# Decode attention with a gated MLP: gate moved into the attention output, MLP part summed in PSUM, result gathered on 8 partitions and stored by two transfers, last weight piece halved

## The chip, the cores and the metric

The kernel runs on one core of one Trainium2 chip. The metric is the time of one execution in device microseconds (us), as a median of several. In the trace of one execution the span is about 1.8 us shorter than that time (190.2 for 191.94 us, for example). A ratio is the mean time of one kernel's fast runs over the mean of the fast runs of the kernel before of the same rounds, on the same chip; so it is not quite the ratio of the medians that are quoted beside it. The interval after a ratio is a 95% one. "Same" means within 2%.

## The reference

Eight sequences decode one token each. One input row x gives a gate, an attention result over the last 1024 positions of a key and value cache, and an MLP result; the output mixes the two.

```python
def reference(A_x, A_k_cache, A_v_cache, A_wq, A_wo, B_x, B_w1, B_b1, B_w2, B_b2, gate_w):
    x = A_x                                               # [8, 1, 448], bf16
    g = _sigmoid((x * gate_w).sum(-1, keepdims=True))     # one number per sequence
    a = _A_ref(x, A_k_cache, A_v_cache, A_wq, A_wo)       # attention: 16 heads of 256, 8 kv heads,
                                                          # then o [8, 4096] @ wo [4096, 448]
    b = _B_ref(x, B_w1, B_b1, B_w2, B_b2)                 # layernorm, 448 -> 1792, gelu, -> 448
    return g * a + (1 - g) * b
```

## The kernel before

All large inputs (77.7 MB) stream through a ring of nine landing buffers of 128 partitions x 16,384 bytes. SP issues all these loads. The buffers lie in SBUF behind the pool of constants, so each tile added to that pool moves them.

```python
    WO_PARTS = [[(0, NJ8)]] * (NHQ - 1) + [[(0, 4), (4, 6), (6, 8)]]
    ...
    consts = ctx.enter_context(tc.tile_pool(name="consts", bufs=1))
    ring = ctx.enter_context(tc.tile_pool(name="ring", bufs=RING))      # RING = 9, SLOT = 8192 bf16
    ...
    def pump():
        while len(slots) < min(len(plan), consumed[0] + RING):
            t = ring.tile([P, SLOT], BF16, tag="slot", name="slot")
            plan[len(slots)](t)
            slots.append(t)
```

The last load is the output projection `wo`; its last quarter comes in the pieces that `WO_PARTS` names, so that only a small piece is left when the stream ends. The result has 8 rows and 448 columns. The projection uses four column tiles of the matmul array at once: block i of 112 columns appears on partitions 32i to 32i+7 of one PSUM tile.

```python
    def tiles(ps):
        return [
            (ps[32 * i : 32 * i + NB, :], slice(i * DO, (i + 1) * DO))   # NB = 8, DO = 112
            for i in range(OT)                                           # OT = 4
        ]
    ...
    nc.vector.memset(A_ps[:], 0.0)
    ...
    def project(q):
        w = slot("wo", q - q % 2)
        for j in range(NJ8):
            o = ((q % 2) * NJ8 + j) * D
            for dst, cols in tiles(A_ps):
                nc.tensor.matmul(dst, lhsT=oP[:, j, q, :], rhs=w[:, o + cols.start : o + cols.stop],
                                 start=(q == 0 and j == 0), stop=(q == NHQ - 1 and j == NJ8 - 1))
    ...
    nc.vector.scalar_tensor_tensor(          # res = A_ps * gate + mixb, all 128 partitions at once
        res[:], in0=A_ps[:], scalar=gg_s[:, 0:1], in1=mixb[:], op0=ALU.mult, op1=ALU.add)
    for i, (src, cols) in enumerate(tiles(res)):
        eng = nc.sync if i % 2 == 0 else nc.scalar
        eng.dma_start(out_f[:, cols], src)   # four stores of 8 rows x 224 bytes, two a queue
```

`mixb` holds (1 - g) times the MLP result, ready long before the end.

## Time and profile before

| | before |
|---|---|
| time, median | 192.38 us (first three runs), 192.34 us (six runs) |
| load queue | 77.67 MB, 96.7% of the time of 16 DMA engines |
| last weight piece usable by the matmul engine (PE) | 186.55 us |
| last store landed | 189.13 us |
| end of the span | 190.17 us |

The first fence is from the profile page of the kernel before: the share of time that the DMA engines were busy and their rate, in 40 equal slices of the span; then the queues (packets, MB, share of 16 engines' time); then the shares of the chain of waits that ended last.

```profile
DMA  5999999999999999999999999999999999999990
GB/s 194 413 424 428 426 431 433 427 420 427 427 434 420 431 417 441 424 424 434 424 431 429 424 420 438 424 427 424 427 434 434 420 420 431 431 431 420 409 373 26
...
q1 hardware_dynamic: 6512, 77.67, 96.7%
q8 instruction: 8, 0.13, 0.3%
...
q14 instruction: 4, 0.03, 0.0%
...
DMA 77%; PE 12%; DVE 7%; SPq 1%; ACT 1%; issue 1%
```

The loads run at a constant rate from the second slice to the end, and the chain is mostly DMA. So the time is the load stream, plus what comes after its last byte. The Trainium skill, "DMA: Bandwidth & Descriptors", section "Where 436 GB/s comes from", gives 435.2 GB/s as the ceiling of the path into SBUF; this trace, at some 427 GB/s, agrees.

The second fence is the timeline of the end: start, duration, engine, line, operation, and in brackets the idle time before it and what ended it.

```profile
186.55 0.36 PE L671 MATMUL A_ps<-slot,oP 128*8 128x112 bf16 x8 [0.21 <-DMA slot<-in_A_wo_dram]
186.55 0.10 PEld L671 LDWEIGHTS <-oP 128*8 128x8 bf16 x7 [0.40 <-issue]
186.96 0.33 DVE L689 SCALAR_TENSOR_TENSOR res<-A_ps,gg_s,mixb 128x112 bf16<-128x112 f32 x1 [3.73 <-PE A_ps L671]
187.32 0.71 SPq L699 DMA_DIRECT2D out_dram<-res  x2
187.33 0.65 ACTq L699 DMA_DIRECT2D out_dram<-res  x2
```

After the last weight piece come 8 matmuls, one operation on VectorE (DVE), and two store issues on each of two queues. The third fence is the same kernel's waits of SP's queue at the end (total, times, longest).

```profile
SPq L725 <- DMA out_dram<-res: 1.1, 2, 0.9
```

SP waited 0.9 us for a store's landing at the end.

### The profile page before, as it was taken

To read this page: it belongs to the slowest core of one execution; us is meant where nothing else is said; L and a number is where in the kernel's file an instruction comes from. 1 tells how busy PE (TensorE), PEld (TensorE's weight loads), DVE (VectorE), ACT (ScalarE), POOL (GpSimd) and SP (SyncE) were. 2 spreads that over 40 slices of the span, in tenths; PEclk is the share of its full clock that TensorE was granted. 3 is DMA by queue.
4 is the path that set the end of the run, shared out by engine and by line. 5 is a ranking of instruction groups with operands and counts; after the bars stand their busy time and mean duration, and the time that the engine had idled before them with its cause. 6 is when DMAs were issued, how large, how long until landed. Compare 5 with 4: busy or idle time off the path is not lost.

```text
span 190.2 us, 2502 instructions
## 1 busy us (share of the span) xinstructions
PE 128.5 (68%) x1013; PEld 67.1 (35%) x1022; DVE 128.0 (67%) x186; ACT 43.1 (23%) x91; POOL 5.0 (3%) x7
## 2 busy tenths in 40 slices
PE   0037799896848775796669874848396839687572
PEld 0021783442413342344234433324142414244261
DVE  7866256798949494949494949495868677685300
ACT  2030230034030404040403140404022400335200
POOL 8100000000000000000000000000000000000000
PEclk9999999999996999699975999999799987999555
DMA  5999999999999999999999999999999999999990
GB/s 194 413 424 428 426 431 433 427 420 427 427 434 420 431 417 441 424 424 434 424 431 429 424 420 438 424 427 424 427 434 434 420 420 431 431 431 420 409 373 26
DMA packets 6734, 77.85 MB, mean 409 GB/s; under 512 B 945, under 2 KB 1346, under 8 KB 1986
## 3 DMA queue, kind: packets, MB, share of 16 engines
q1 hardware_dynamic: 6512, 77.67, 96.7%
q8 instruction: 8, 0.13, 0.3%
q10 hardware_dynamic: 210, 0.02, 0.1%
q14 instruction: 4, 0.03, 0.0%
HBM read 77.68 MB, written 0.01 MB: 409 GB/s over the span
## 4 chain that ended last, share of the span: by engine, by line
DMA 77%; PE 12%; DVE 7%; SPq 1%; ACT 1%; issue 1%
DMA slot<-in_A_k_cache_dram 40%; DMA slot<-in_A_v_cache_dram 20%; DMA slot<-in_A_wo_dram 10%; DMA slot<-in_A_wq_dram 7%; PE S L428 6%; DVE kt L356 5%; PE hT L553 2%; PE hT L543 1%; DVE mx L440 1%; SPq L118 1%; SPq L134 1%; PE Sq L370 1%; PE qt L385 1%; ACT qs L380 1%; PE qp L398 1%
## 5 line engine op out<-in xcount | busy, mean ns | idle before, releaser
L356 DVE STREAM_TRANSPOSE kt<-slot 128x2048 int32<-128x2048 int32 x32 | 73.7, 2306 | 34.4 <-DMA slot<-in_A_k_cache_dram 34.4
L428 PE MATMUL S<-kt,qw 128*128 128x512 bf16 x256 | 70.2, 421 | 34.5 <-DVE kt L356 30.1
L428 PEld LDWEIGHTS <-qw 128*128 128x128 bf16 x256 | 26.5, 104 | 71.9 <-issue 51.1
L457 ACT ACTIVATE E<-S,nmx 128x1024 bf16<-128x1024 f32 x16 | 22.2, 1387 | 2.5 <-DVE nmx L454 2.5
L533 ACT CAST oT<-fin 128x16 bf16<-128x16 f32 x16 | 3.6, 226 | 78.7 <-PE fin L530 78.7
L440 DVE TENSOR_REDUCE mx<-S 128x1 f32<-128x1024 f32 x16 | 19.0, 1187 | 1.2 <-PE S L428 1.2
L500 PE MATMUL PO<-slot,ET 128*16 128x512 bf16 x256 | 18.3, 410 | 1.4 <-DMA slot<-in_A_v_cache_dram 1.4
L509 ACT ACTIVATE first<-PO,own 128x256 f32<-128x256 f32 x16 | 7.6, 473 | 28.2 <-PE PO L500 28.2
L470 DVE STREAM_TRANSPOSE ET<-E 128x512 int32<-128x512 int32 x16 | 11.2, 698 | 2.2 <-ACT E L457 2.2
L422 PE MATMUL S<-place,foreign 128*128 128x512 bf16 x23 | 9.2, 400 | 0.1
L448 PE MATMUL mz<-m,same 128*128 128x4 f32 x32 | 6.2, 265 | 4.1 <-ACT oT L533 4.1
L481 PEld LDWEIGHTS den<-rowsum,rowden 128*128 128x128 f32 x32 | 6.7, 214 | 3.3 <-issue 1.0
L500 PEld LDWEIGHTS <-ET 128*16 128x16 bf16 x256 | 5.3, 91 | 6.0 <-issue 2.3
L448 PEld LDWEIGHTS mz<-m,same 128*128 128x128 f32 x32 | 5.0, 195 | 6.0 <-ACT oT L533 5.3
L422 PEld LDWEIGHTS <-foreign 128*128 128x128 bf16 x32 | 3.2, 100 | 8.5 <-issue 6.7
L481 PE MATMUL den<-rowsum,rowden 128*128 128x1 f32 x32 | 5.0, 226 | 0.4 <-ACT E L457 0.4
L370 PE MATMUL Sq<-slot,xT 128*8 128x512 bf16 x32 | 3.9, 615 | 1.9 <-DMA slot<-in_A_wq_dram 1.9
L413 DVE CAST qw<-qp 32x512 bf16<-32x512 f32 x4 | 2.8, 688 | 3.4 <-ACT qw L411 3.4
L492 ACT ACTIVATE rsel<-sel,rb 128x8 f32<-128x8 f32 x16 | 4.7, 297 | 1.1 <-DVE rb L491 1.1
L671 PE MATMUL A_ps<-slot,oP 128*8 128x112 bf16 x128 | 4.0, 290 | 1.2 <-DMA slot<-in_A_wo_dram 1.2
L291 POOL MEMSET qw<- 128x5120 bf16 x1 | 4.4, 4364 | 0.0
L442 DVE TENSOR_SCALAR m<-block,mx 128x4 f32<-128x4 f32 x16 | 3.7, 230 | 0.6
(135 smaller groups left out, 81.7 us busy)
## 6 DMA issues: line engine op xcount, KB each, us to landing
slot<-in_A_v_cache_dram SPq DMA_DIRECT2D x16, 2048.0 KB, 36.2
slot<-in_A_k_cache_dram SPq DMA_DIRECT2D x15, 2048.0 KB, 39.1
slot<-in_A_wo_dram SPq DMA_DIRECT2D x3, 896.0 KB, 31.0
slot<-in_A_k_cache_dram SPq DMA_DIRECT2D x2, 1024.0 KB, 7.4
slot<-in_A_wq_dram SPq DMA_DIRECT2D x1, 2048.0 KB, 11.7
slot<-in_B_w_dram SPq DMA_DIRECT2D x1, 1568.0 KB
slot<-in_B_w_dram SPq DMA_DIRECT2D x1, 1344.0 KB
slot<-in_A_wq_dram SPq DMA_DIRECT2D x1, 1024.0 KB, 13.5
```

Source lines behind the costliest of these rows:

```text
L356: nc.vector.transpose(kt[:].rearrange("p c k x r -> p (c k x r)").bitcast(WORD), kn[:, hf * CH * Dh : (hf + 1) * CH * Dh].bitcast(WORD),)
L370: nc.tensor.matmul(Sq[32 * t : 32 * t + NB, n * QN : (n + 1) * QN], lhsT=xT[:, r + half, :], rhs=w[:, o + c : o + c + QN], start=(r == 0), ...
L422: nc.tensor.matmul(S[u][:, cols], lhsT=foreign[:], rhs=place[:], start=True, stop=False)
L428: nc.tensor.matmul(S[u][:, cols], lhsT=qw[:, j, u, m * RQ : m * RQ + P], rhs=kt[:, :, k, :, par], start=False, stop=(k == NK - 1 and par = ...
L440: nc.vector.reduce_max(mx[:], S[u][:], axis=AXIS.X)
L448: nc.tensor.matmul(mz[:], lhsT=same[:], rhs=m4[:], start=True, stop=True)
L457: nc.scalar.activation(E[:].rearrange("p c x i -> p c i x"), S.pop(u)[:].rearrange("p (c i x) -> p c i x", i=PAIR, x=BLK), ACT.Exp, bias=n ...
L470: nc.vector.transpose(ET[:].rearrange("p c r i -> p (c r i)").bitcast(WORD), E[:].rearrange("p c x i -> p (c x i)").bitcast(WORD),)
L481: nc.tensor.matmul(den[u][:], lhsT=rowden[:], rhs=rowsum[:], start=True, stop=True)
L492: nc.scalar.activation(rsel[u][:], sel2[:], ACT.Copy, scale=rb[:])
L500: nc.tensor.matmul(PO[32 * t : 32 * t + PAIR * RQ], lhsT=ET[:, c, 0:RQ, :], rhs=vn[:, PAIR * c * Dh : PAIR * (c + 1) * Dh], start=(c < QUA ...
L509: nc.scalar.activation(first[:], PO[:, 0, :], ACT.Copy, scale=own[:, 0:1])
```

## The change

The intent is a shorter way out after the last byte. The gate is multiplied into each attention unit's output by the copy that is there anyway. The MLP part is put into the accumulator by an identity matmul before the projection. The result then needs only a cast, done by DVE and ScalarE (ACT) for two blocks each, into a tile of 8 partitions, which two wider stores send off, one a queue. The last weight piece is one matmul group instead of two. The gate's new broadcast (a tile `each` and a second small matmul) and the reuse of two MLP tiles are cut here.

```diff
-    WO_PARTS = [[(0, NJ8)]] * (NHQ - 1) + [[(0, 4), (4, 6), (6, 8)]]
+    WO_PARTS = [[(0, NJ8)]] * (NHQ - 1) + [[(0, 4), (4, 7), (7, 8)]]
 ...
-    gg_s = consts.tile([P, 2], F32)
+    gg_s = consts.tile([P, 1 + NB], F32)
+    ident_f = consts.tile([P, P], F32)
+    each = consts.tile([NB, NB + P], F32)
 ...
-    res = consts.tile([P, DO], BF16)
+    res = consts.tile([NB, D], BF16)
+    nc.vector.tensor_copy(ident_f[:], ident[:])
 ...
-        nc.scalar.copy(
-            oT[:, half * RQ : (half + 1) * RQ, :, b].rearrange("p h j -> p j h"), sm[:]
+        nc.scalar.activation(
+            oT[:, half * RQ : (half + 1) * RQ, :, b].rearrange("p h j -> p j h"),
+            sm[:],
+            ACT.Copy,
+            scale=gg_s[:, 1 + b : 2 + b],
         )
 ...
-    nc.vector.memset(A_ps[:], 0.0)
+    nc.tensor.matmul(
+        A_ps[:], lhsT=ident_f[:], rhs=mixb[:], start=True, stop=False, skip_group_check=True
+    )
 ...
-                    start=(q == 0 and j == 0),
+                    start=False,
                     stop=(q == NHQ - 1 and j == NJ8 - 1),
+                    skip_group_check=True,
 ...
-    nc.vector.scalar_tensor_tensor(
-        res[:],
-        in0=A_ps[:],
-        scalar=gg_s[:, 0:1],
-        in1=mixb[:],
-        op0=ALU.mult,
-        op1=ALU.add,
-    )
-    for i, (src, cols) in enumerate(tiles(res)):
-        eng = nc.sync if i % 2 == 0 else nc.scalar
-        eng.dma_start(out_f[:, cols], src)
+    for i, (src, cols) in enumerate(tiles(A_ps)):
+        if i < OT // 2:
+            nc.vector.tensor_copy(res[:, cols], src)
+        else:
+            nc.scalar.copy(res[:, cols], src)
+    for eng, cols in ((nc.sync, slice(0, D // 2)), (nc.scalar, slice(D // 2, D))):
+        eng.dma_start(out_f[:, cols], res[:, cols])
```

More of the change, by code (lines that the diff above doesn't have):

```diff
@@ L339, in norm_and_gate @@
         )
-        gp = ps_misc.tile([P, 2], F32, tag="misc", name="gp")
+        nc.vector.memset(each[:], 1.0)
+        nc.vector.tensor_scalar_mul(each[:, 0:NB], ident[0:NB, 0:NB], gg[:, 0:1])
+        gp = ps_misc.tile([P, 1 + NB], F32, tag="misc", name="gp")
         nc.tensor.matmul(
-            gp[:],
+            gp[:, 0:1],
             lhsT=spread[:].rearrange("p i b -> p (i b)"),
-            rhs=gg[:],
+            rhs=gg[:, 1:2],
             start=True,
             stop=True,
+        )
+        nc.tensor.matmul(
+            gp[:, 1 : 1 + NB], lhsT=each[:, NB : NB + P], rhs=each[:, 0:NB], start=True, stop=True
         )
@@ L570, in mlp_hidden @@
         nc.vector.tensor_tensor(z2[:], z[:], z[:], op=ALU.mult)
-        uu = consts.tile([P, NF, NB], F32)
+        uu = z2
         nc.vector.tensor_scalar(
@@ L578, in mlp_hidden @@
         nc.scalar.activation(th[:], w_[:], ACT.Tanh, scale=0.7978845608028654)
-        hh = consts.tile([P, NF, NB], F32)
+        hh = th
         nc.vector.tensor_scalar(hh[:], th[:], 1.0, 0.5, op0=ALU.add, op1=ALU.mult)
@@ L602, in mlp_out @@
         done()
-        nc.scalar.activation(mixb[:], bb[:], ACT.Copy, scale=gg_s[:, 1:2])
+        nc.scalar.activation(mixb[:], bb[:], ACT.Copy, scale=gg_s[:, 0:1])
     norm_and_gate()
@@ L646 @@
     invert(u)
-    nc.vector.memset(A_ps[:], 0.0)
+    nc.tensor.matmul(
+        A_ps[:], lhsT=ident_f[:], rhs=mixb[:], start=True, stop=False, skip_group_check=True
+    )
     oP = consts.tile([P, NJ8, NHQ, NB], BF16)
```

## The prediction

> **What bounds the kernel now.** The load stream. The page's slices show the DMA engines fully busy from the second slice to the last but one, at about 427 GB/s (77.67 MB on the load queue). The Trainium skill, "DMA: Bandwidth & Descriptors", section "Where 436 GB/s comes from", puts the ceiling of the path into SBUF at 435.2 GB/s; this trace agrees. The chain of waits is 77% DMA. PE (68% busy) and DVE (67%) wait for it: DVE sat idle 34.4 us for key tiles.
>
> So two things count: whatever would let the stream run dry, and the tail after the last byte. The timeline there: last weight piece usable by PE at 186.55; 8 matmuls, 0.36; DVE combine of result, gate and MLP part at 186.96, 0.33; two store issues on each of SP and ACT from 187.32, 0.71 the pair; store packets about 0.95 after their issue starts; end at 190.2.
>
> **What the change does, by place.**
>
> 1. Head: a 128x128 cast (about 0.23, like the copies of that size), a small memset and an 8x8 multiply (0.16, 0.15), a second small FP32 matmul (0.5 with its loads). DVE reaches the first key transpose about 0.5 us later. By then 17 MB of loads are queued and about 7 MB moved, so the stream does not run dry: 0.
>
> 2. Per unit, the copy of the attention output becomes a scaled copy. The 128x16 cast takes 226 ns, a scaled 128x8 one 297: +0.07 us x 16 on ACT, which is 23% busy. In the last unit it is done over 1 us before its weight piece lands: 0.
>
> 3. The accumulator's memset (0.15) becomes an FP32 identity matmul, about 0.5 us at the half clock granted there. It falls ahead of a PE wait of 1.02 us for values: 0.
>
> 4. Last piece 896 B instead of 1792 B a row, bytes the same. In the packet records 1792 B take 74 ns, 896 B 41; 2688 B I estimate at 107. A DMA engine has 8 rows of each: 8 x (74 + 74) = 8 x (107 + 41) = 1.18 us. The last byte lands at the same time, but 4 matmuls remain behind it, not 8; four column tiles overlap, so one step: -0.08 us.
>
> 5. The combine (0.33 on DVE) becomes two 8x112 copies on DVE beside two on ACT: about 0.27 and 0.30 each, 0.46 and 0.52 a pair with overlap (estimates from 128x128, 128x16 and 128x112 operations): +0.19 us.
>
> 6. Stores: one issue a queue instead of two, so the last issue starts right after the copy, not 0.34 later: -0.34 us.
>
> Sum: -0.08 + 0.19 - 0.34 = -0.23 us of 192.38. I predict **192.13 us**, 8 in 10 between 191.8 and 192.45; faster by over 2%: 0.5%, within 2%: 99%, slower: 0.5%.
>
> **What would show it.** Slices still near 427 GB/s; last weight usable within 0.1 us of before; four matmuls after it; ACT's second copy ending about 0.52 us after PE; one store issue a queue, near 187.4; end near 189.95.
>
> **What would make it wrong.** An instruction fetch (8 KB, 0.3 us on one DMA engine at 185.8, in the packet records) moving against the last load: 0.2 us either way. Copies that start late on ACT or don't overlap: the gain of the single issue is gone. The larger piece's 12 matmuls not done when the last piece lands: the 0.08 is lost. The end may hang on something fixed other than the last issue.

## The result, and the profile after

| | before | after |
|---|---|---|
| time, median of six runs | 192.34 us (192.03 to 192.42) | 193.39 us (193.30 to 193.60) |
| ratio | | 1.0058 [1.0045, 1.0071], class same |
| last weight piece usable by PE | 186.55 | 187.46 |
| from the start of the last projection matmul to the last store's landing | 2.52 | 2.68 |
| from that landing to the end | 1.04 | 1.58 |

The result is correct. It is 1.05 us slower where 0.23 us of gain was predicted, and outside the predicted range. From the page of the kernel after, the lines that answer to those of before:

```profile
DMA  5999999999999999999999999999999999999970
GB/s 196 416 412 439 423 419 432 420 420 438 431 420 434 417 427 434 420 427 431 420 434 429 417 431 427 427 427 420 431 427 420 434 427 424 431 426 415 406 307 3
...
q1 hardware_dynamic: 6496, 77.67, 96.1%
q8 instruction: 8, 0.13, 0.3%
...
q14 instruction: 4, 0.03, 0.0%
...
DMA 96%; SPq 1%; issue 0%; PE 0%; ACT 0%; DVEq 0%; DVE 0%; ACTq 0%
```

The stream still looks full in every slice; the bytes are the same. At this resolution nothing is to be seen of the first surprise, that the last piece came 0.91 us later. The timeline of the end of the kernel after:

```profile
187.17 0.55 PE L684 MATMUL A_ps<-slot,oP 128*8 128x112 bf16 x16 [0.32 <-DMA slot<-in_A_wo_dram]
187.18 0.37 PEld L684 LDWEIGHTS <-oP 128*8 128x8 bf16 x15 [0.50 <-issue]
187.75 0.56 DVE L705 CAST res<-A_ps 8x112 bf16<-8x112 f32 x2 [3.71 <-PE A_ps L684]
188.34 0.37 SPq L709 DMA_DIRECT2D out_dram<-res  x1
188.40 0.50 ACT L707 CAST res<-A_ps 8x112 bf16<-8x112 f32 x2 [5.37 <-DVE res L705]
188.94 0.30 ACTq L709 DMA_DIRECT2D out_dram<-res  x1
```

The second surprise is in the fifth line: ACT's copies start at 188.40, after DVE's two are done, and the bracket says that ACT was released by DVE and not by PE. The view of waits says it once more, and the view of SP's queue has a longer wait for the stores:

```profile
ACT res L707 <- DVE res L705: 5.4, 1, 5.4
```

```profile
SPq L735 <- DMA out_dram<-res: 1.4, 1, 1.4
```

The third surprise is not in any of these views. It is in the table above: the end comes 1.58 us after the last landing, not 1.04. The raw records of SP show where (start in us, duration in ns; each entry waits for the semaphores of one or two queues, here after all stores had landed at 190.15):

```
after    190.167   17  event semaphore
         190.625   28  event semaphore      <- 0.44 us of nothing before it
         190.708   27  event semaphore
         190.778   28  event semaphore
before   188.939   28  event semaphore
         189.145   28  event semaphore      <- the last landing was at 189.129
         189.214   28  event semaphore
         189.281   28  event semaphore
```

So there are three things to explain: ACT behind DVE, a later last byte, and a pause in SP at the end.

### The profile page after: what moved, and what is told of

It is laid out like the page before. It is cut to its first block, busy times and chain, and to the rows that moved or that the text cites. A ratio compares the mean times of both kernels' runs of the same rounds, so it can differ in the third digit from the quotient of the medians.

```text
span 191.7 us, 2514 instructions
## 1 busy us (share of the span) xinstructions
PE 132.8 (69%) x1017; PEld 69.4 (36%) x1026; DVE 128.6 (67%) x189; ACT 45.1 (24%) x93; POOL 5.0 (3%) x7
## 4 chain that ended last, share of the span: by engine, by line
DMA 96%; SPq 1%; issue 0%; PE 0%; ACT 0%; DVEq 0%; DVE 0%; ACTq 0%
DMA slot<-in_A_k_cache_dram 77%; DMA slot<-in_A_wo_dram 12%; DMA slot<-in_A_wq_dram 7%; SPq L118 1%; SPq L134 0%; PE A_ps L684 0%; ACT res L707 0%; DVEq L735 0%; DVE res L705 0%; ACTq L707 0%
## 5 line engine op out<-in xcount | busy, mean ns | idle before, releaser
L541 ACT ACTIVATE oT<-fin,gg_s 128x16 bf16<-128x16 f32 x16 | 5.3, 329 | 76.8 <-PE fin L538 76.8
L508 PE MATMUL PO<-slot,ET 128*16 128x512 bf16 x256 | 20.0, 441 | 1.1 <-DMA slot<-in_A_v_cache_dram 1.1
L462 DVE TENSOR_REDUCE nmx<-mz 128x1 f32<-128x4 f32 x16 | 2.3, 143 | 3.1 <-PE mz L456 3.1
```

What stands on the lines that cost most here:

```text
L508: nc.tensor.matmul(PO[32 * t : 32 * t + PAIR * RQ], lhsT=ET[:, c, 0:RQ, :], rhs=vn[:, PAIR * c * Dh : PAIR * (c + 1) * Dh], start=(c < QUA ...
L541: nc.scalar.activation(oT[:, half * RQ : (half + 1) * RQ, :, b].rearrange("p h j -> p j h"), sm[:], ACT.Copy, scale=gg_s[:, 1 + b : 2 + b],)
```

## The experiments

The theories, and their rivals, were these.

- **Copies.** ACT is chained behind DVE because both read the same PSUM tile. (Rival: ACT is simply late, or slow to start.) In the compiled program ACT's first copy waits for the count that DVE reaches with its second copy, and builds that were not run showed that two result tiles, or one PSUM tile over two banks, leave this wait in, while two PSUM tiles take it out.
- **Last byte.** The new constants moved the landing buffers in SBUF by 864 bytes, and the address sets the time of a packet. (Rival: scatter between executions; or the halved piece.)
- **Pause.** It hangs on the number of final waits, or on the two wide stores, or on a position in SP's program.

Where a number is "after the last matmul", it is counted from the start of the last projection matmul in that run's trace. This is not quite the moment at which the last weight piece becomes usable: in the kernel before, where two matmul groups are left, it comes 0.06 us later, in the kernel after, with one group left, 0.01. Where the halved piece counts, the text therefore says "from the last piece".

### Controls: both kernels again

No edit. The first run shows how large a difference of nothing is.

> The kernel before, unedited, as a control. Both theories: ratio 1.000 within 0.001. It also gives a second trace of before. In the first pair of traces the last weight was usable by PE at 186.55 us before and the very last piece at 187.46 after, 0.9 apart, more than the whole difference of the medians (1.05) leaves beside a tail that is 0.65 longer. Theory T (tail: the copies are chained, and the end of the program grew): that landing varies by some tenths of a us between executions of one kernel. Theory L (load stream: layout, head or split slow it): the landing here is within 0.15 us of 186.55.

Measured: 192.28 us, ratio 0.9989 [0.9975, 1.0003]. Last landing 2.52 after the last matmul, end 3.56. So a ratio that differs from 1 by 0.001 says nothing.

> The changed kernel, unedited, as a control. Ratio 1.005 to 1.007. Theory T: the time from the last weight's matmuls to the end of the span is again about 4.2 us against 3.6 before, and the landing of the last weight comes within 0.5 us of before's. Theory L: the landing is again 0.9 us later than before's.

Measured: 193.75 us, ratio 1.0055 [1.0042, 1.0068]; 2.63 and 4.21. The loss repeats on another chip, and so do the chained copies and the pause. In this pair the last load landed at 186.84 (before) and 187.22 (after).

### Copies: e1, the accumulator in two PSUM tiles

```diff
-    A_ps = ps_misc.tile([P, DO], F32, tag="misc", name="A_ps")
+    A_ps0 = ps_misc.tile([P, DO], F32, tag="misc", name="A_ps0")
+    A_ps1 = ps_s.tile([P, W], F32, tag="S", name="A_ps1")
+    # blocks 0 and 1 (read by DVE) in A_ps0, blocks 2 and 3 (read by ACT) in A_ps1; both seeded
```

> The changed kernel with the accumulator in two PSUM tiles, columns 0 and 1 in one, 2 and 3 in the other, so that the program no longer has ACT's copies wait for DVE's. Theory T: ACT's two copies start within 0.1 us of DVE's first instead of 0.65 after it, the last store issue starts 0.55 to 0.65 us earlier, and the time falls by about 0.6 us against the changed kernel (ratio to before about 1.0025). Theory L: the copies overlap too, but the time stays within 0.2 us of the changed kernel, because the late landing is what was paid for.

Measured: 193.25 us, ratio 1.0032 [1.0019, 1.0044]. The timeline of its end:

```profile
187.80 0.54 DVE L715 CAST res<-A_ps 8x112 bf16<-8x112 f32 x2 [4.28 <-PE A_ps L694]
187.84 0.50 ACT L717 CAST res<-A_ps 8x112 bf16<-8x112 f32 x2 [5.34 <-PE A_ps L694]
188.37 0.37 SPq L719 DMA_DIRECT2D out_dram<-res  x1
188.37 0.30 ACTq L719 DMA_DIRECT2D out_dram<-res  x1
```

ACT is now released by PE, both engines copy side by side, and both stores are issued at 188.37. The last landing comes 2.30 us after the last matmul: 0.38 less than in the kernel after. From the last piece it is 2.31, against 2.58 in the kernel before: 0.27 less, where the prediction's tail had promised 0.23. The end comes 3.87 after the last matmul; the pause is still there (1.57 from landing to end). So the chain of the two engines cost about 0.4 us, and it is shown. It was expected to cost 0.6, and the copies do end 0.61 us sooner; but with both stores issued at once SP's lands last, 1.44 us after its issue began, where it took 1.25 in the kernel after. The Trainium skill, "PSUM — Partial Sum Buffer", section "PSUM bank collisions raise a hardware error", says that two engines may access different quadrants of one bank at the same time. The four blocks lie in four quadrants; the wait was put in all the same by the framework, which guards the tile.

### The old way out in the new kernel: e2

```diff
-    for i, (src, cols) in enumerate(tiles(A_ps)): ... two copies on DVE, two on ACT, two stores
+    nc.vector.tensor_copy(res[:], A_ps[:])
+    for i, (src, cols) in enumerate(tiles(res)):
+        eng = nc.sync if i % 2 == 0 else nc.scalar
+        eng.dma_start(out_f[:, cols], src)
```

> The changed kernel with before's way out: one 128x112 DVE copy of the accumulator to 32-spaced partitions and four stores. Head, gate in the attention output, seed of the accumulator and the halved last piece stay as changed. Theory T: the time returns to before's, 192.2 to 192.4 (ratio 0.999 to 1.000). Theory L: it stays near the changed kernel, ratio 1.004 or more.

Measured: 192.36 us, ratio 0.9991 [0.9978, 1.0004]; last landing 2.41 after the last matmul, end 3.44 (0.12 less than before, from the halved piece and a plain cast). From its timeline:

```profile
187.72 0.27 DVE L703 CAST res<-A_ps 128x112 bf16<-128x112 f32 x1 [3.70 <-PE A_ps L684]
188.02 0.71 SPq L706 DMA_DIRECT2D out_dram<-res  x2
188.02 0.65 ACTq L706 DMA_DIRECT2D out_dram<-res  x2
```

All the rest of the change (the gate in the attention output, the identity matmul, the halved piece) is in this kernel, and the loss is gone. So these parts cost nothing that can be seen, as predicted, and the loss is tied to the new way out (and, in part, to what it does to addresses, below: `res` is smaller here).

### The halved piece alone: e3

```diff
-    WO_PARTS = [[(0, NJ8)]] * (NHQ - 1) + [[(0, 4), (4, 6), (6, 8)]]
+    WO_PARTS = [[(0, NJ8)]] * (NHQ - 1) + [[(0, 4), (4, 7), (7, 8)]]
```

> The kernel before with the last weight piece halved and nothing else. The prediction's step 4: four matmuls instead of eight behind the last landing, so DVE starts about 0.28 us after the last piece's first matmul rather than 0.35, about 0.1 us in all, ratio 0.9995; no change in the landing of the last weight beyond the scatter of 0.3 us. If the 896-byte packets cost more than estimated, the last weight lands later by 0.2 us or more and the ratio is over 1.001.

Measured: 192.21 us, ratio 0.999 [0.9976, 1.0005]. From the last matmul group to DVE's start 0.31 us instead of 0.35, end 3.51 instead of 3.56. From the last piece to DVE's start it is 0.32 us instead of 0.41, so the gain is 0.09, and 0.08 was predicted; the ratio is within the scatter that the control showed.

### Last byte: e4, e5 and e10, dead bytes in front of the landing buffers

Each of these adds one constant tile that nothing reads; only the addresses of the landing buffers change. e4 does this to the kernel after, e5 and e10 to the kernel before.

```diff
     res = consts.tile([NB, D], BF16)            # e4; e5 and e10 have the old res here
+    consts.tile([P, 8], F32, name="pad")        # 32 bytes in e4 and e5; [P, 32], 128 bytes, in e10
```

> The changed kernel with one dead 32-byte constant, which moves the nine landing buffers from an address of 32 modulo 64 back to a multiple of 64 (44000 to 44032; before had 43136). The nearly undisturbed 16 KB load packets took 614.5 ns on average in both traces of before and 615.6 in all three of the changed kernel and its first variant. Theory A (alignment): the mean returns to 614.8 or less, the last weight lands 0.3 us earlier, the time falls by 0.3 us against the changed kernel, to a ratio of about 1.004. Rival (the packet mean follows something else, such as the added instructions): it stays at 615.6 and the time with it.

Measured: 191.64 us, ratio 0.9963 [0.995, 0.9976]. The kernel after, with nothing but 32 dead bytes, was faster than the kernel before. About 0.3 us was expected; by the ratios (1.0056 to 0.9963) it was about 1.8.

> The kernel before with the same dead 32 bytes, which moves its landing buffers to 32 modulo 64 (43136 to 43168) and changes nothing else. Theory A: packet mean 615.6 ns, time 0.3 us up, ratio about 1.0015. Rival: 614.5 ns and ratio 1.000 within 0.001.

Measured: 192.5 us, ratio 1.0016 [1.0, 1.0033]. The ratio alone would fit the theory of a 64-byte boundary (1.0015 expected); what speaks against it is the packet mean, 614.5 ns where it expected 615.6.

> The kernel before with 128 dead bytes, which moves its landing buffers from 128 modulo 256 to a multiple of 256 that is not one of 512 (43136 to 43264). The packet mean was 614.5 ns at 128 and at 160 modulo 256, 614.8 at 64, 615.6 at 224, and 611.0 at 0. Theory A2 (a multiple of 256 saves 3.5 ns a packet): mean 611.0 ns, the last weight lands 0.9 us earlier, ratio about 0.995. Rival (it needs a multiple of 512, or the saving belongs to the changed kernel): 614.5 ns and 1.000.

Measured: 190.73 us, ratio 0.9919 [0.9903, 0.9935]. The page of e10, for the rate by slice:

```profile
GB/s 192 423 425 434 429 436 429 420 427 434 444 420 427 434 434 427 423 434 441 427 423 425 441 441 416 434 430 434 423 430 434 437 420 434 427 434 421 421 376 31
```

The slices are too coarse for a difference of under 1%. The packet records are not. This table has the start of the landing buffers (from the compiled program; they are 16,384 bytes apart) modulo 256, and the mean time of one full load packet of 16,384 bytes on a DMA engine (the few over 700 ns, 8 to 20 of 4,096 in a trace, left out):

| landing buffers start at, mod 256 | kernels | mean packet, ns |
|---|---|---|
| 0 | e4, e8, e9, e10, e12 to e15, e17 | 611.0 |
| 64 | e2 | 614.8 |
| 128 | before, c1, e3, e7 | 614.4 to 614.5 |
| 160 | e5 | 614.5 |
| 224 | after, c2, e1, e11, e16 | 615.6 |

The mean repeats to 0.1 ns between executions and chips at a given address. 16 engines with a packet of 611.0 ns make 429.0 GB/s, with 615.6 ns 425.8 GB/s. e10 (256 but not 512) and e4 (512) are alike, so 256 bytes is what counts. The Trainium skill, "DMA: Bandwidth & Descriptors", section "How a descriptor splits into AXI transactions", says that a descriptor (one piece of a transfer) that doesn't start on a 256-byte boundary also fetches the unused bytes before its start, and that they take bus beats; its text and table are about the bytes read. Here it was the side written that was off the boundary, and it cost 3.5 to 4.6 ns a packet.

The change moved the buffers from 128 to 224: 1.1 ns on each of 256 such packets an engine, about 0.3 us. The busy time of the load queue per engine, 183.46 in c1 and 183.80 in c2, agrees (0.34). The landing of the last load scatters by some tenths between executions of one kernel (186.51 to 186.84 in four profiles of kernels with buffers at 128), so the 0.91 us between the first two profiles is partly scatter. The timed runs give an estimate without it: a ratio of 1.0056 (between the two comparisons, 1.0058 and 1.0055) is 1.08 us, and the way from the last piece to the end grew by 0.63 (3.62 to 4.25, the means of two profiles each), which leaves 0.45 us for the last byte. Packets, busy time and this remainder agree on 0.3 to 0.45; no run takes this step of the address by itself. A second rival stays untested: the queue q8 sends an instruction packet of 16,384 bytes among the last loads, 1.13 us long from 185.31 in the kernel before and 1.20 us long from 186.18 in the kernel after; how much it held back the last piece isn't known. The whole step to 256 was measured: from c1 to e10 the end of the last load packet moved from 186.35 to 184.90 us. 256 packets of 3.5 ns are 0.9 us of that 1.45; smaller packets gained too (12,544 bytes: 477.1 ns in the kernel after, 469.0 in e8); the rest is open.

### The pause: e7, is it the number of final waits?

SP waits at the end for 11 semaphores in the kernel before and for 12 in the kernel after. e7 gives the kernel before a twelfth.

```diff
     for q in range(1, NHQ):
         project(q)
 
+    spare = ps_sm.tile([P, QUAD], F32, tag="sm", name="spare")
+    nc.tensor.matmul(spare[:], lhsT=ident[:], rhs=ident[:, 0:QUAD], start=True, stop=True)
```

> The kernel before with one small matmul after the last projection whose result nobody reads, so that the program's final wait has twelve semaphores in place of eleven, as in the changed kernel. The matmul runs beside DVE's combine. Theory W (the number of final waits makes the pause): SP pauses about 0.46 us after its first final wait, the time from the last store's landing to the end goes from 1.04 to 1.58 us, ratio about 1.0028. Rival (the pause comes with the 448-byte stores or with one store a queue): 1.04 us, ratio 1.000.

Measured: 192.3 us, ratio 0.9999 [0.9986, 1.0012]; from the last landing to the end 1.03. No pause, so the number of waits is not it.

### All causes undone but the pause: e8

```diff
 # on the kernel after, with the 32 dead bytes of e4:
-    A_ps = ps_misc.tile([P, DO], F32, tag="misc", name="A_ps")
+    A_v0 = ps_misc.tile([P, DO], F32, tag="misc", name="A_v0")      # block 0, read by DVE
+    A_v1 = ps_s.tile([P, W], F32, tag="S", name="A_v1")             # block 1, read by DVE
+    A_s = ps_s.tile([P, W], F32, tag="S", name="A_s")               # blocks 2 and 3, read by ACT
```

> The changed kernel with all three suspected costs undone at once: three PSUM tiles, so that ACT does not wait for DVE and DVE's last copy is the only one that waits for the last matmul, which brings the final wait back to eleven semaphores; and the dead 32 bytes for the address. If chained copies, final wait and address are all of it, the last store lands 2.30 us after the last weight's first matmul (before 2.52), the end follows 1.04 later, and the time is 0.2 us under before's, ratio 0.9988, the -0.23 us of the prediction. If a part of the cause is missing, the ratio stays above 1.0005.

Measured: 191.17 us, ratio 0.9941 [0.9929, 0.9953]. The copies are free (last landing 2.23 after the last matmul), the packets take 611.0 ns, the final waits are 11, and still the end comes 1.51 us after the last landing. The copies and the address are independent of the pause.

### A no-op on SP: e9 and e11

```diff
+    nc.sync.nop(nofuse=True)          # near the start; e9 on e8, e11 on the kernel after
     pump()
     nc.scalar.dma_start(x_sb[:], xf)
```

> The kernel of e8_all_undone with one no-operation added at the start of SP's program. In every trace so far a pause of 0.44 to 0.46 us stood between SP's 79th and 80th recorded instruction when those two were final waits (one store on SP), and could not be seen when the 79th was a store and the 80th a wait for it (two stores on SP). Theory P (position in SP's instruction stream): the pause moves one instruction ahead, to between the store and the first final wait, where it is hidden behind the landing; the end follows the last landing by 1.04 to 1.08 us in place of 1.51, ratio about 0.992. Rival (the pause belongs to a first final wait that lasts about 1 us or to having one store on SP): 1.5 us and 0.994 again.

Measured: 191.34 us, ratio 0.9948 [0.993, 0.9966]; landing to end 1.51.

> The changed kernel with the same one no-operation on SP. Theory P: the end follows the last landing by about 1.1 us in place of 1.58, time 0.45 us under the changed kernel's, ratio 1.003. Rival: 1.58 us and ratio 1.0055.

Measured: 193.71 us, ratio 1.0084 [1.0051, 1.0117]; landing to end 1.57. Two of its six runs took 195.1 us, among them the profiled one. There PE reached its last work late: from 160 to 180 us it had a granted clock of 0.74, where the kernel after had 0.95 in the same stretch. As the program is that of the kernel after, this is a difference between executions; its cause is open.

The pause did not move. The no-op doesn't appear among SP's records, and the programs of e9 and e8, and those of e11 and the kernel after, came out the same byte for byte on every engine. The no-op was dropped in the build, so these two runs are repeats and say nothing of a position. They do show how far one program scatters: the kernel after measured 1.0058, 1.0055 and, as e11, 1.0084, beyond the intervals of the first two.

### The stores: e12 to e15

By now the pause had appeared in all seven profiles of kernels with two wide stores and in none of the seven with four narrow ones. Four kernels change only who issues what.

```diff
 # e12, on e8: four stores of 8 x 224 bytes, two on SP, two on ACT
-    for eng, cols in ((nc.sync, slice(0, D // 2)), (nc.scalar, slice(D // 2, D))):
-        eng.dma_start(out_f[:, cols], res[:, cols])
+    for i in range(OT):
+        cols = slice(i * DO, (i + 1) * DO)
+        eng = nc.sync if i < OT // 2 else nc.scalar
+        eng.dma_start(out_f[:, cols], res[:, cols])
 # e13, on e8: both wide stores on SP
-    for eng, cols in ((nc.sync, slice(0, D // 2)), (nc.scalar, slice(D // 2, D))):
+    for eng, cols in ((nc.sync, slice(0, D // 2)), (nc.sync, slice(D // 2, D))):
 # e14, on e8: both wide stores on ACT
+    for eng, cols in ((nc.scalar, slice(0, D // 2)), (nc.scalar, slice(D // 2, D))):
 # e15, on e10: the old tail with one store on SP and three on ACT
-        eng = nc.sync if i % 2 == 0 else nc.scalar
+        eng = nc.sync if i == 0 else nc.scalar
```

> The kernel of e8 (parallel copies, aligned buffers, new tail) with four 224-byte-row stores, two on SP and two on ACT, instead of two of 448. Theory S (the pause hangs on the stores: their number or row size): last landing to end back from 1.51 to about 1.04 us; last landing about 0.35 us later than e8 because of the second issue a queue (2.55 after the last matmul); total about 0.1 us below e8, 0.9935 of before. Rival R (the pause comes from other parts of the new tail, such as the copies on two engines or the eight-partition result): still 1.5 us, total about 0.35 us above e8, 0.996.

Measured: 191.57 us, ratio 0.9963 [0.9938, 0.9988]; landing to end 1.03, but the last landing 3.28 after the last matmul, where 2.55 was expected.

> e8 with both wide stores issued by SP, none by ACT at the end. Theory Q (the pause hangs on SP having issued only one store): pause gone, last landing to end about 1.04 us. Theory N (it hangs on two wide stores rather than four narrow ones, whichever queue): still about 1.5 us. Either way the last landing comes 0.1 to 0.35 us later than in e8 (2.3 to 2.6 us after the last matmul) because SP issues twice.

Measured: 192.25 us, ratio 0.9991 [0.996, 1.0022]; landing to end 1.08, last landing 3.67 after the last matmul, where 2.3 to 2.6 was expected.

> e8 with both wide stores issued by ACT and none by SP. Theory Q (one or fewer stores on SP brings the pause): pause still there or longer, landing to end 1.5 us or more. Theory N (two wide stores): still about 1.5 us. If the pause is gone here and in e13, it hangs on two queues being used once each, which neither theory says. Last landing about 2.6 us after the last matmul, since both issues wait for ACT's copies.

Measured: 191.25 us, ratio 0.9954 [0.9919, 0.9988]; landing to end 1.52, last landing 2.42.

> The aligned old kernel (e10) with its four narrow stores kept, one issued by SP and three by ACT. Theory Q (one store on SP): the pause of about 0.45 us appears, landing to end 1.5 us instead of 1.03. Theory N (store width and count): no pause, 1.03 us. In both the last landing comes about 0.35 us later than e10 (2.85 after the last matmul), because ACT issues three times; total by N about 0.35 us above e10, by Q about 0.8.

Measured: 191.06 us, ratio 0.993 [0.9903, 0.9956]; landing to end 1.22, last landing 2.61.

None of the theories fits: in e12 and e13 the pause seems gone, but the landings are late; in e15 it is there in part. The timeline of e12 shows where it went:

```profile
185.93 1.17 SPq L723 DMA_DIRECT2D out_dram<-res  x2
185.95 0.69 ACTq L723 DMA_DIRECT2D out_dram<-res  x2
```

Two issues take ACT 0.69 us and SP 1.17. In the kernel before it was 0.65 and 0.71. The pause has moved in between SP's two issues. So we counted SP's entries in the trace from its first, in all kernels, and the pause stands in the same place in each of them, after the 79th:

| kernel | 79th entry of SP | 80th entry of SP | time between them, us | what it delayed |
|---|---|---|---|---|
| after | first final wait | second final wait | 0.441 | the end |
| e1 | first final wait | second final wait | 0.436 | the end |
| e8 | first final wait | second final wait | 0.442 | the end |
| e12 | wait for a semaphore | second store issue | 0.445 | a store |
| e13 | wait for a semaphore | second store issue | 0.442 | a store |
| e14 | third final wait | fourth final wait | 0.450 | the end |
| e15 | first final wait | second final wait | 0.436 | partly hidden: the last landing was 0.173 before its end |
| before | second store issue | first final wait | 0.905 | nothing: the 80th entry waited for a landing |
| e2 | second store issue | first final wait | 0.891 | nothing, likewise |
| e10 | second store issue | first final wait | 0.911 | nothing, likewise |

The count is of entries in the trace. A branch at the end of the body leaves no entry; counted with it, in the compiled program, the place in e12 and e13 is one instruction earlier than in after, e1, e8, e14 and e15, and the reason is not known. With two stores on SP and one wait in front of them, the old tail has its second issue as the 79th entry, and the 80th is a wait of 0.9 us for landings anyway. With one store on SP the pause comes one step later, among the final waits, where nothing hides it.

### One more instruction on SP, early: e16 and e17

If it is the place that counts, one more entry on SP far ahead of the end must move the pause back into the wait for the landings. Splitting one early weight load in two does this and touches nothing of the end.

```diff
 # e16 on the kernel after, e17 on e8
-    WO_PARTS = [[(0, NJ8)]] * (NHQ - 1) + [[(0, 4), (4, 7), (7, 8)]]
+    WO_PARTS = [[(0, 4), (4, 8)]] + [[(0, NJ8)]] * (NHQ - 2) + [[(0, 4), (4, 7), (7, 8)]]
```

> The changed kernel with one weight load of SP split in two, some 15 us before the end, so that every later instruction of SP stands one place later; stores, copies and buffers unchanged. Theory O (the pause stands at a fixed place in SP's program): it now falls between the store's issue and the first final wait, in time that SP waits for the landing anyway; last landing to end from 1.58 to between 1.04 and 1.10 us, last landing still 2.65 after the last matmul; ratio to before 1.0033 instead of 1.0056. Theory N (two wide stores bring the pause): nothing changes, 1.58 us and 1.0056.

Measured: 194.01 us, ratio 1.0087 [1.0074, 1.0101]. The last landing to the end took 1.10 us, as expected of the place; the 79th entry is now the store's issue, and the 80th waits for a landing. But the last landing came 3.49 us after the last matmul, not 2.65, and the kernel was slower than ever. The packet records of the end (start in us, duration in ns, of the eight rows of ACT's store and of one other packet):

```
189.780   25   store, 448 bytes
189.787   33   store, 448 bytes
189.789   34   store, 448 bytes
189.801   22   store, 448 bytes
189.817   24   store, 448 bytes
189.820   24   store, 448 bytes
189.841   26   store, 448 bytes
189.861  324   instruction queue, 8192 bytes, on one DMA engine
190.181   25   store, 448 bytes       <- landed at 191.023, the other seven by 190.332
```

The eighth row's packet starts just as a packet of q14 ends, one of the two queues that the page calls "instruction", and landed 0.69 us late; that both were on the same engine is inferred from this, since the kept trace names no engine. This packet is tied to the pause: in 16 of the 20 profiles that were looked at it starts 1.05 to 1.09 us after the end of SP's 79th entry (in the four others up to 0.3 us later). Moving the pause forward moved the packet forward too, into the store. The same packet held up one row of SP's second store in e12 (502 ns; that row landed 0.59 us after the others) and in e13 (548 ns; 0.63 us), which is why their landings came late beyond the pause itself.

> The same split load in e8 (ScalarE free of VectorE, aligned buffers). Theory O: last landing to end 1.04 instead of 1.51 us, end about 3.27 us after the last matmul, ratio to before 0.9917 instead of 0.9941; this would be the prediction's tail with all three unforeseen terms away. Theory N: 1.51 us, 0.9941.

Measured: 190.82 us, ratio 0.9925 [0.9911, 0.9938]. The last landing to the end took 1.13 us instead of e8's 1.51, and the end came 3.40 after the last matmul instead of 3.74. Here ACT's store is issued 0.6 us earlier than in e16 and is gone by the time the packet comes (188.12). The gain is 0.34 us in the trace, less than the 0.47 expected, because where there is no pause there are still some 0.04 us between two waits, the step after the first was 0.09 and not 0.07, and the landing itself came 0.04 later than in e8.

So the place in SP's program decides, and it is shown by the three kinds of entry before which it stood (a final wait, a store's issue, a wait hidden by a landing) and by moving it on purpose. That the pause is a wait for instructions is inferred: from the fixed place, and from the instruction packet that follows it at a fixed distance. The Trainium skill, "Runtime: NRT & Kernel Launch", section "Instruction fetch mechanics", says that the sequencer fetches the next block by its own DMA queue while it runs the current one, in blocks of 16 KiB, and that the cost is mostly hidden. These traces show packets of 16,384 bytes on q8, which agrees, but packets of 8,192 bytes on q14, whose last packet follows the pause, and 0.44 us that is hidden only where SP waits anyway.

e10 (0.9919) and e17 (0.9925) are the fastest kernels run. Their intervals overlap. A kernel with e10's addresses, free copies, and both the pause and the packet away from the stores is close to e17 already; nothing better was run.

## Why the prediction was right or wrong

Predicted was -0.23 us; measured was +1.05. The step that failed is the prediction's step 5, "two 8x112 copies on DVE beside two on ACT": sized at 0.52 us for a pair with overlap, the four copies took 1.15 us one engine after the other, because ACT was made to wait for DVE, and 0.38 us of the delay came through to the last landing. Two more parts failed. In step 4, "The last byte lands at the same time" did not hold (0.3 to 0.45 us later, worked out). And step 6 saved its issue as predicted, but the sum left the path from the last landing to the end as it was, and that path grew by 0.54 us, the largest of the three.

| term | predicted | shown | by |
|---|---|---|---|
| steps 1 to 3 (head, scaled copies, identity matmul) | 0 | nothing seen | e2, ratio 0.9991 with all of them in |
| step 4, halved piece: one matmul group less | -0.08 | -0.09 from the last piece to DVE's start | e3 |
| step 4, "the last byte lands at the same time" | 0 | +0.3 to +0.45, worked out | packet means 614.5 and 615.6 ns; what the tail leaves of the ratio |
| step 5, copies | +0.19 | +0.21 where they overlap (e1: 0.54 for 0.33); chained, 0.38 more at the landing | e1: landing at 2.30 instead of 2.68 |
| step 6, one issue a queue | -0.34 | -0.37, for the landing | first store issue to last landing: 1.81 in before, 1.44 in e1 |
| SP's pause no longer hidden, with one more wait | not foreseen | +0.54 | after, e8, e14 against before, e16, e17 |

The sum of the prediction and the three misses is -0.23 + 0.38 + 0.54 + 0.35 = +1.04, against +1.05 measured. It is no more exact than its terms: the last one is worked out and may be 0.3 or 0.45, so the near-perfect match is partly luck.

- **What bounds the kernel.** Right. The stream sets the time, and the largest gain over the kernel before came with 0.6% off the time of a packet (e10), which nobody had planned.
- **Copies side by side.** Wrong, and settled. The two took turns: 1.15 us from the start of DVE's first copy to the end of ACT's second, where DVE alone had needed 0.33. The prediction had named the risk ("copies that start late on ACT or don't overlap") but gave it no weight in the sum. The wait could have been read from the compiled program.
- **One issue a queue.** The mechanism was right: with the chain away (e1), the last landing comes 0.27 us earlier after the last piece than before. But taking one issue off SP brought the unseen pause from a place where SP waited anyway to one where it did not. The prediction's last sentence, that the end may hang on something fixed other than the last issue, was the right worry.
- **Same last byte.** Wrong. The prediction counted bytes and packets and not where they land; the new constants moved the buffers. How much of the later landing in the first pair of profiles is this, and how much is scatter, is not settled beyond the 0.3 to 0.45 us worked out above.
- **The instruction packet.** The prediction feared one at 185.8 us against the last load. That one is the third of four on q14 while the kernel runs; in the kernel after the third comes at 167.80, far from the last load, so it can't have made the last piece late. The one that did harm was the next, and it did it in the experiments e12, e13 and e16, not in the kernel after (there it came at 191.26, behind all stores).

Left open: what the pause is made of, the part of e10's and e4's gain beyond the packet arithmetic, and e11's two slow runs.

## What to carry to other kernels

When a kernel is bound by a stream of loads, look first at the start addresses of the landing buffers modulo 256: adding or dropping any small constant moves them; here that outweighed the whole change to the last microseconds. When two engines are to share the last step, give each its own PSUM tile and check in the trace's bracket who released the second. When instructions are taken off a queue, ask what was hidden behind them: count the entries of SP at the end in both traces before believing in a gain of tenths of a microsecond.

## What the Trainium skill lacked or had wrong

- "DMA: Bandwidth & Descriptors", "How a descriptor splits into AXI transactions": it speaks of reads. The start of the written SBUF row matters as well: a 16,384-byte packet took 611.0 ns at a multiple of 256, some 614.5 at 128 and 160, 614.8 at 64 and 615.6 at 224. In the kernel before, aligning it made 0.8% of the whole time (e10).
- "Runtime: NRT & Kernel Launch", "Instruction fetch mechanics": it gives blocks of 16 KiB and calls the cost mostly hidden. Packets of 16,384 bytes are seen here on q8, but those on q14 have 8,192 bytes, and SP has a pause of 0.436 to 0.450 us at a fixed place of its program (after its 79th entry in the trace), which adds to the time where SP doesn't wait for anything else. That this pause is an instruction fetch is inferred.
- No page gives a figure for how long such a packet, 324 to 548 ns on one DMA engine, holds up a small store: one row landed 0.59 to 0.69 us behind the others (e12, e13, e16).
- "PSUM — Partial Sum Buffer", "PSUM bank collisions raise a hardware error": different quadrants are free for two engines, but the page doesn't say that the framework still orders two engines that read one tile, in different quadrants (or, in a build that was not run, in different banks). It cost 0.38 us here (e1).
